# Soft MoE after chunked attention on one core: the scores in two buffers instead of one, and another order of the first loads

## The chip, the core and the metric

The kernel runs on one core of a Trainium2 chip. The core has five engines, each with its own queue of instructions: TensorE (PE, matrix products; PEld is its loading of weights, which overlaps PE), VectorE (DVE), ScalarE (ACT), GpSimd (POOL) and SyncE (SP), which here issues every DMA. [...] The metric is the device time of one execution in microseconds, as the median of several runs.

## The reference

Three stages are computed one after the other, in float32.

```
# 1. attention in chunks of 64: q, k, v are (8, 8, 576, 64)
scores = q_c @ k_c.T / 8 ; attn = softmax(scores) ; x = attn @ v_c      # x: 4608 x 512
# 2. soft MoE: phi 512 x 32, 8 experts with 4 slots each, F = 1024
logits = x @ phi
d = softmax over tokens(logits) ; slots = d.T @ x
slot_out[e] = relu(slots[e] @ w1[e]) @ w2[e]
x = softmax over slots(logits) @ slot_out
# 3. solu block: w_in 512 x 1024, w_out 1024 x 512
h = x @ w_in ; solu = h * softmax(h) ; ln = (solu - mean) / sqrt(var + 1e-6) * g_ln
out = ln @ w_out
```

## The kernel before

The 4608 tokens are 36 tiles of 128 (NT). The first part goes through 36 steps; step i does the attention of tile i and, in the same turn, parts of older tiles. In each step stand, among others:

- `S` (pe_S, L256): eight products of q and k give the scores of tile i, 128 x 512, one PSUM bank. Even steps use one half of the tile `sx`, odd steps the other.
- `mx` (L265) and `sub` (L271) on VectorE: the row maxima, and the scores less the maxima, into SBUF. After `sub` the bank is free again.
- `exp` (L277) on ScalarE; `PT` and `PTe` (L407, L398) transpose the result of the step before on TensorE and copy it out.
- `x` (L282): the product with the values, two steps behind; `rz`, `rc`, `xm` (L304, L483, L487): its sums, their reciprocals, and the scaled x, which frees the two banks of the x tile.
- `xT`, `xTe`, `LT`, `L`, `sl` and others: the transposed x, the logits of a block of four tiles, and the running sums of stage 2.
- `t`, `sq`, `u`, `a`, `m`, `add`, `mul`: from step 2 on, one of 32 conversions a step. The words of w_in and w_out are read as 64-bit pieces (`raw`) and rounded. `t` and `sq` (L210, L206) run on ScalarE, `u` and `a` (L213, L223) on VectorE, `m`, `add`, `mul` (L219, L229, L233) on GpSimd. There is one buffer for what `sq` writes, so `sq` of the next conversion waits for `mul` of this one.

The order of all this is written out by hand in `STEP`, one line for each step modulo 4; each engine executes its share in that order and doesn't overtake. Loads are asked for in the same order on SyncE: `qk` asks for q and k four steps ahead, in two DMAs of 256 KB, `v` for a pair of value tiles (520 KB), `raw` for a pair of words tiles (512 KB), `W` for tiles of the experts' weights (512 KB) as `PACE` says. A DMA waits until the one eight before it has landed. What is asked for before the first step is listed in `FIRST`. Later the hand-written list `ORDER` leads from the last tiles through stage 2 (`x34` uses both halves of `sx` for the values' product of tile 34) into stage 3, which runs tile after tile to the end.

## Time and profile before

| | us |
|---|---|
| median of 3 runs (lowest to highest) | 403.69 (403.28 to 404.21) |
| the profiled execution, its own time | 402.77 |
| span of that execution, first to last instruction | 401.0 |
| PE busy in the span | 382.4 (95%) |
| DVE busy | 311.0 (78%) |
| ACT busy | 224.3 (56%) |
| POOL busy | 200.2 (50%) |

The profile comes from one execution. Its span is 1.77 us shorter than its time, and that time is 0.92 us below the median. Busy shares are means over parts of quite different kinds: attention and conversions until about 124 us, the experts until about 184, the last block until the end. Matrix products are pipelined and their ends are modelled, so two products may overlap in a listing. In every listing, what stands in brackets behind a row is the idle time of that engine just before, and what ended it.

### The profile page before, as it was taken

The page shows a single profiled execution, that of the slowest core. Times are in us where ns is not written, and L with a number is a line of the kernel's source. Part 1 is how long each engine was busy: PE and PEld are TensorE (multiplying, and loading weights), DVE is VectorE, ACT ScalarE, POOL GpSimd, SP SyncE. Part 2 cuts the span into 40 slices and gives each one's busy share as a digit, 9 for nine tenths or more (in the row PEclk, how much of TensorE's full clock was granted, in tenths as well). Part 3 has the DMA queues.
Part 4 walks back from the last instruction along what each step waited for, and adds up shares of the span by engine and source line. Part 5 has one row for each costly group of instructions (what it writes and reads, how often), then busy time and mean ns, then how long its engine had stood idle before and what let it go on. Part 6 is the DMA issues. An engine that isn't in the chain of part 4 may idle for free. (4 is left out here: it accounts for less than half of the span.)

```text
span 401.0 us, 10317 instructions
## 1 busy us (share of the span) xinstructions
PE 382.4 (95%) x3947; PEld 220.4 (55%) x3947; DVE 311.0 (78%) x777; ACT 224.3 (56%) x470; POOL 200.2 (50%) x201
## 2 busy tenths in 40 slices
PE   3799899999999999999999999999999999999997
PEld 2577777777787642354544444444444444444445
DVE  3788788989886449574989799999888888888840
ACT  1577877877785512332577765556554555455521
POOL 2577767777778246330123255555455544454430
PEclk9999999999999999999999999999999999999999
DMA  7999999999999999991156757777665666557671
GB/s 231 403 409 408 389 397 397 409 407 407 410 397 408 401 396 406 409 391 26 30 103 146 140 134 159 159 158 148 144 140 135 144 151 133 132 137 158 132 159 52
DMA packets 101153, 99.20 MB, mean 247 GB/s; under 512 B 78064, under 2 KB 78704, under 8 KB 101104
## 3 DMA queue, kind: packets, MB, share of 16 engines
q1 hardware_dynamic: 101104, 98.54, 77.1%
q8 instruction: 31, 0.51, 0.5%
q14 instruction: 18, 0.15, 0.1%
HBM read 70.60 MB, written 9.44 MB: 200 GB/s over the span
## 5 line engine op out<-in xcount | busy, mean ns | idle before, releaser
L1194 POOL TENSOR_SCALAR uh<-u,sc 128x1024 f16<-128x1024 f32 (+1 forms) x35 | 65.1, 1860 | 51.1 <-issue 38.3
L1393 PEld LDWEIGHTS <-uhT 128*128 128x128 f16 x560 | 52.1, 98 | 68.3 <-issue 8.8
L1393 PE MATMUL o_ps<-xb,uhT 128*128 128x512 f16 x280 | 66.7, 380 | 0.7 <-DMA uhT<-uh 0.7
L1393 PE MATMUL o_ps<-xb,ulT 128*128 128x512 f16 x280 | 66.3, 379 | 0.0
L1393 PE MATMUL o_ps<-wo,uhT 128*128 128x512 f16 x280 | 66.1, 379 | 0.0
L1322 ACT ACTIVATE e<-h_ps,nm 128x1024 f32<-128x1024 f32 x34 | 37.8, 1113 | 43.7 <-DVE nm L1316 43.7
L1210 ACT ACTIVATE e<-u,nmean 128x1024 f32<-128x1024 f32 x35 | 40.1, 1147 | 28.7 <-DVE nmean L1209 28.7
L256 PE MATMUL s_ps<-qk 128*64 128x128 f32 x576 | 41.1, 287 | 9.3 <-DMA qk<-in_qkT 6.5
L1360 POOL TENSOR_TENSOR a<-a,mhalf 128x1 f32<-128x1 f32 x36 | 21.8, 606 | 56.2 <-DVE a L1377 42.5
L1316 DVE TENSOR_REDUCE nm<-h_ps 128x1 f32<-128x1024 f32 x34 | 41.5, 1220 | 9.3 <-PE h_ps L1311 9.3
L1185 DVE SCALAR_TENSOR_TENSOR u<-h_ps,e 128x1024 f32<-128x1024 f32 x35 | 42.8, 1223 | 6.1 <-ACT e L1322 6.1
L1393 PEld LDWEIGHTS <-ulT 128*128 128x128 f16 x280 | 27.3, 98 | 33.1 <-issue 0.3
L1370 DVE SCALAR_TENSOR_TENSOR ul<-u,sc,uh 128x1024 f16<-128x1024 f32 x35 | 45.3, 1295 | 0.0
L256 PEld LDWEIGHTS s_ps<-qk 128*64 128x64 f32 x576 | 32.5, 141 | 16.2 <-issue 10.3
L398 ACT ACTIVATE xt_b<-xt_ps 128x512 f32<-128x512 f32 (+1 forms) x37 | 21.6, 586 | 17.8 <-PE xt_ps L416 16.9
L265 DVE TENSOR_REDUCE mx<-s_ps 128x8 f32<-128x512 f32 x36 | 24.6, 684 | 8.5 <-PE s_ps L256 8.0
L1411 ACT ACTIVATE ob<-o_ps,a 128x512 f32<-128x512 f32 x35 | 23.8, 679 | 9.3 <-PE o_ps L1393 8.0
L219 POOL TENSOR_SCALAR conv<-conv 128x256 f32<-128x256 f32 x16 | 17.6, 1099 | 21.8 <-ACT conv L206 21.8
L1311 PE MATMUL h_ps<-s,c4T 128*128 128x512 f32 x68 | 27.4, 485 | 0.0
L277 ACT ACTIVATE p<-p 128x512 f32<-128x512 f32 x35 | 21.7, 621 | 6.6 <-DVE p L271 6.6
L271 DVE TENSOR_TENSOR p<-s_ps,mx 128x512 f32<-128x512 f32 x35 | 24.1, 690 | 0.9
L229 POOL TENSOR_TENSOR conv<-conv 128x256 int32<-128x256 int32 x32 | 23.3, 729 | 2.6
(232 smaller groups left out, 633.5 us busy)
## 6 DMA issues: line engine op xcount, KB each, us to landing
w<-in_w SPq DMA_DIRECT2D x45, 512.0 KB, 8.0
qk<-in_qkT SPq DMA_DIRECT2D x72, 256.0 KB, 6.8
vall<-in_v SPq DMA_DIRECT2D x18, 520.0 KB, 6.7
out<-ob SPq DMA_DIRECT2D x35, 256.0 KB, 2.1
raw<-in_w SPq DMA_DIRECT2D x16, 512.0 KB, 6.4
qk<-in_w SPq DMA_DIRECT2D x4, 512.0 KB, 9.0
w_raw<-in_w SPq DMA_DIRECT2D x3, 512.0 KB, 9.0
vall<-in_w SPq DMA_DIRECT2D x3, 512.0 KB, 8.9
```

Of the source, the lines that this page charges most:

```text
L256: nc.tensor.matmul(s[ts(c, 64), ts(g, 128)], b[:, 1, ts(2 * g + c, 64)], b[:, 0:3:2, ts(2 * g + c, 64)], start=True, stop=True, tile_posit ...
L265: mark("mx", nc.vector.tensor_reduce(out=mx, in_=s, axis=AX.X, op=ALU.max))
L271: mark("sub", nc.vector.tensor_tensor(out=p, in0=s, in1=mx.unsqueeze(2).to_broadcast([128, 8, 64]), op=ALU.subtract,))
L1185: nc.vector.scalar_tensor_tensor(out=u, in0=d["h"], scalar=1.0, in1=e, op0=ALU.mult, op1=ALU.mult, accum_out=zz[:, 1:2])
L1194: nc.gpsimd.tensor_scalar(out=uh[:, 0:n], in0=u[:, 0:n], scalar1=d["sc"][:, 1:2], scalar2=1.0, op0=ALU.mult, op1=ALU.mult)
L1210: nc.scalar.activation(out=d["e"], in_=d["u"], func=AF.Square, bias=nmean, scale=1.0, accum_out=d["zz"][:, 2:3])
L1311: nc.tensor.matmul(h[:, ts(n, 512)], c4T[:, i, :], s4[n], start=True, stop=True)
L1316: nc.vector.tensor_reduce(out=nm, in_=st[i]["h"], axis=AX.X, op=ALU.max, negate=True)
L1322: nc.scalar.activation(out=d["e"], in_=d["h"], func=AF.Exp, bias=d["nm"], scale=1.0, accum_out=d["zz"][:, 0:1])
L1370: nc.vector.scalar_tensor_tensor(out=ul, in0=d["u"], scalar=d["sc"][:, 1:2], in1=d["uh"], op0=ALU.mult, op1=ALU.subtract)
L1393: nc.tensor.matmul(d["o"], lt(n % 8), w(n % 8), start=(n == 0), stop=(n == 23))
L1411: nc.scalar.activation(out=ob, in_=d["o"], func=AF.Copy, scale=d["a"][:, 7:8])
```

## The change

The score tile with two halves becomes two tiles in a pool of their own. The pool is closed before `x34`, which opens a new one with one tile over two banks; that one is closed before the experts' stage opens its own PSUM pool. In FIRST, q and k of step 3 stand behind g and phi, and the second pair of values and the second and third words are taken out. They are asked for in the `qk` operation of steps 0 and 1 instead, behind q and k of steps 4 and 5. In two lines of STEP `v` moves behind `qk`.

```
-S a x u raw v m qk rz sl mx t W rc z xT sub xTe PT PTe add xm acc mul sq exp
+S a x u raw m qk v rz sl mx t W rc z xT sub xTe PT PTe add xm acc mul sq exp
...
-FIRST = "cs qk0 qk1 qk2 v0 raw0 qk3 g phi v2 raw2 raw4"
+FIRST = "cs qk0 qk1 qk2 v0 raw0 g phi qk3"
+THEN = {0: 'v2 raw2', 1: 'raw4'}
...
-    sx = ps1.tile([128, 2, 512], F32, name="s_ps")
+    pss = ctx.enter_context(ExitStack())
+    ps_s = pool("ps_s", 1, pss, space=PSUM)
+    s_banks = [ps_s.tile([128, 512], F32, name="s_ps", tag=f"s{a}") for a in range(2)]
+    sx = None
 
     def pe_S(i):
-        s = sx[:, i % 2, :]
+        s = s_banks[i % 2]
...
+        def q():
+            load_qk(i + 4)
+            for o in THEN.get(i, "").split():
+                first_loads[o]()
+
...
-            S=(True, lambda: pe_S(i)), qk=(True, lambda: load_qk(i + 4)),
+            S=(True, lambda: pe_S(i)), qk=(True, q),
...
     def x34():
+        nonlocal sx
+        pss.close()
+        sx = pool("ps_sx", 1, pss, space=PSUM).tile([128, 2, 512], F32, name="s_ps")
         xps_t[n - 1] = x = sx
...
     def open_2():
         nonlocal e1, ps2, soT, cz, mx
+        pss.close()
         p1.close()
```

SyncE, from the first load to those of step 2, before. The names ending in 111 to 114 are the four buffers of q and k; 111 is that of steps 0 and 4.

```order
L241 DMA cs_60<-in_cst 128x257
L176 DMA qk0_111<-in_qkT 64x1024 x2
L176 DMA qk1_112<-in_qkT 64x1024 x2
L176 DMA qk2_113<-in_qkT 64x1024 x2
L181 DMA vall_123<-in_v1 128x1040
L189 DMA raw_137<-in_w64 128x1024
L176 DMA qk3_114<-in_qkT 64x1024 x2
L242 DMA g_sb_62<-in_g_ln 128x8
L241 DMA phi_sb_61<-in_phi 128x128
L181 DMA vall_123<-in_v1 128x1040
L189 DMA raw_144<-in_w64 128x1024
L189 DMA raw_146<-in_w64 128x1024
...
```

The same place of the changed kernel, from the first words on:

```order
L190 DMA raw_137<-in_w64 128x1024
L243 DMA g_sb_62<-in_g_ln 128x8
L242 DMA phi_sb_61<-in_phi 128x128
L177 DMA qk3_114<-in_qkT 64x1024 x2
L177 DMA qk0_111<-in_qkT 64x1024 x2
L182 DMA vall_123<-in_v1 128x1040
L190 DMA raw_165<-in_w64 128x1024
L177 DMA qk1_112<-in_qkT 64x1024 x2
L190 DMA raw_182<-in_w64 128x1024
L182 DMA vall_123<-in_v1 128x1040
```

Up to the first words nothing moved. Behind them q and k of step 4 (the second use of 111) now stand ahead of the second values and words, and those of step 5 ahead of the third words.

TensorE around step 7, before, with the semaphores that an instruction waits for (DVE is that of VectorE, the DMAHW ones those of loads):

```order
L256 MATMUL s_ps<-qk_114 64x128 [waits DMAHW2_49,DMAHW1_49,DVE_49]
L256 MATMUL s_ps<-qk_114 64x128 x7
L282 MATMUL x_ps<-vall,pt 64x65 [waits DVE_49,Activation_49]
L282 MATMUL x_ps<-vall,pt 64x65 x15
L356 MATMUL L_ps<-cs,ltb 128x128 [waits Activation_49]
```

And the same instructions of the changed kernel:

```order
L260 MATMUL s_ps<-qk_114 64x128 [waits DMAHW1_49,DMAHW0_49]
L260 MATMUL s_ps<-qk_114 64x128 x7
L286 MATMUL x_ps<-vall,pt 64x65 [waits DVE_49,Activation_49]
L286 MATMUL x_ps<-vall,pt 64x65 x15
L360 MATMUL L_ps<-cs,ltb 128x128 [waits Activation_49]
```

The order on TensorE is the same; the score products have lost their wait for VectorE, and the product with the values behind them has kept its own.

## Rows read from the trace of the kernel before

**Rows 1.** The page's 40 slices of the span: GB/s moved by the DMA engines.

```profile
GB/s 231 403 409 408 389 397 397 409 407 407 410 397 408 401 396 406 409 391 26 30 103 146 140 134 159 159 158 148 144 140 135 144 151 133 132 137 158 132 159 52
```

**Rows 2.** Busy time in stretches: PE, PEld, DVE, ACT, POOL, PEclk, DMA share, GB/s.

```profile
24.00:48.00 24.00, 22.75 (x451) 17.80 (x442) 19.83 (x47) 18.74 (x49) 18.18 (x22) 1.00 1.02 401
48.00:120.00 72.00, 70.27 (x1399) 55.60 (x1397) 62.99 (x162) 54.63 (x146) 54.58 (x63) 1.00 1.02 403
...
160.00:180.00 20.00, 19.29 (x229) 9.02 (x223) 13.90 (x33) 6.66 (x13) 6.99 (x8) 1.00 1.06 404
```

**Rows 3.** The chain that ended last, its first piece: start, us, what.

```profile
202.85 0.80 DVE nm L1316
```

**Rows 4.** Timeline of SyncE, the last weights: start, us, engine, line, operation, tiles.

```profile
147.82 24.39 SPq L128 DMA_DIRECT2D w<-in_w  x22
```

**Rows 5.** The tile w from 171.8 to 172.0 us: its last load, issue to landing.

```profile
L128 SPq DMA_DIRECT2D w<-in_w x1: 328/328/328, 171.9 to 171.9; - x1
...
DMA to landing us min/median/max: 10.4/10.4/10.4
```

**Rows 6.** Timeline of TensorE where the experts' last products stand.

```profile
182.37 0.33 PE L1047 MATMUL soc_ps<-cs,xb 128*128 128x128 f32 x1 [0.44 <-DVE xb L399]
182.63 1.08 PE L987 MATMUL h_ps<-w,hTb 128*4 128x128 f32 x32
183.50 1.06 PE L1112 MATMUL sw_ps<-wi,soT 128*32 128x512 f32 x8
```

**Rows 7.** Waits, 24 to 120 us (PE, then PEld): us in total, times, longest.

```profile
PE s_ps L256 <- DVE p L271: 0.6, 2, 0.3
...
PEld s_ps L256 <- DVE p L271: 3.1, 11, 0.6
...
PEld s_ps L256 <- issue: 2.2, 12, 0.2
```

**Rows 8.** Timeline of all engines around the score products at 32.7 us.

```profile
32.00 0.69 DVE L271 TENSOR_TENSOR p<-s_ps,mx 128x512 f32<-128x512 f32 x1
...
32.74 0.85 PEld L256 LDWEIGHTS s_ps<-qk 128*64 128x64 f32 x16 [0.59 <-DVE p L271]
...
32.90 0.69 DVE L487 TENSOR_TENSOR xb<-x_ps,rz 128x512 f32<-128x512 f32 x1
...
33.77 0.70 PE L282 MATMUL x_ps<-vall,pt 64*64 64x65 f32 x32
```

**Rows 9.** Timeline of all engines, the first three steps.

```profile
5.16 1.97 PE L256 MATMUL s_ps<-qk 128*64 128x128 f32 x16 [5.16 <-DMA qk<-in_qkT]
...
7.90 0.69 DVE L271 TENSOR_TENSOR p<-s_ps,mx 128x512 f32<-128x512 f32 x1
...
8.69 1.98 PE L256 MATMUL s_ps<-qk 128*64 128x128 f32 x16 [1.56 <-DVE p L271]
...
12.55 0.45 ACT L210 ACTIVATE conv<-raw 128x256 int32<-128x256 uint32 x1 [3.30 <-DMA raw<-in_w]
...
12.90 0.58 ACT L398 ACTIVATE pt<-pt_ps 128x512 f32<-128x512 f32 x1
...
13.89 1.09 POOL L219 TENSOR_SCALAR conv<-conv 128x256 f32<-128x256 f32 x1 [11.20 <-ACT conv L206]
```

**Rows 10.** Timeline of all engines, steps 3 to 5.

```profile
17.57 0.42 ACT L210 ACTIVATE conv<-raw 128x256 int32<-128x256 uint32 x1
...
19.39 1.09 PE L256 MATMUL s_ps<-qk 128*64 128x128 f32 x16 [1.01 <-DMA qk<-in_qkT]
...
20.17 0.44 ACT L206 ACTIVATE conv<-raw 128x256 f32<-128x256 f32 x1 [1.10 <-POOL wi L233]
20.17 0.29 DVE L213 TENSOR_SCALAR conv<-raw 128x256 int32<-128x256 int32 x1 [0.62 <-POOL wi L233]
...
23.94 1.07 POOL L219 TENSOR_SCALAR conv<-conv 128x256 f32<-128x256 f32 x1 [0.57 <-ACT conv L206]
```

**Rows 11.** Line 189 from 9.7 to 10.2 us: the second words, issue to landing.

```profile
L189 SPq DMA_DIRECT2D raw<-in_w x1: 457/457/457, 9.8 to 9.8; - x1
...
DMA to landing us min/median/max: 6.9/6.9/6.9
```

## The prediction

> **What bounds the kernel now.** I read the page's slices first, then the busy time by stage, the chain that ended last, and only then the stretches that the change touches. The slices show the loads at 389 to 410 GB/s from the second slice to the eighteenth and 26 in the nineteenth [rows 1]: the weights stream in without a pause until about 182 us. In the same time TensorE is busy for 22.75 of 24 us, then 70.27 of 72, then 19.29 of 20, with the DMA share above 1.00 throughout [rows 2]. So two resources are full at once up to 182 us. The chain that ended last begins only at 202.85 us [rows 3] and is back-to-back TensorE work from there: nothing in it is touched, and it starts earlier only if the stage before ends earlier.

> That stage ends on weights. SyncE asks for the last 22 tiles without rest from 147.82 us [rows 4]; the last one is asked for at 171.9 and lands 10.4 us later, at 182.3 [rows 5]. TensorE uses the last two tiles in the run that starts at 182.63, just after a wait of 0.44 us for VectorE, and goes on at 183.50 [rows 6]. The run takes 183.50 - 182.63 = 0.87 us, half of it for each tile, so the last tile is used from 183.07. If everything on the engines were early, it could be used from about 182.4: **the whole change can win at most about 0.7 us** as long as the last load lands where it does.

> **The change, part by part.** *Two buffers for the scores.* Before, a score product S of a step waits for the subtraction (L271) of the step just before, because both halves are one tile. Afterwards it needs only the subtraction two steps back, which TensorE's earlier wait for the exponential of that step already covers; so S carries no wait for VectorE in the steps. What that frees is read from the waits between 24 and 120 us: weight loads of S that began after L271 sat idle 11 times for 3.1 us in all, against 12 for 2.2 us where nothing held them, 0.18 us each, which is the ordinary gap. The excess is 3.1 - 11 x 0.18 = 1.1 us. By the matmul records the same wait is 2 times, 0.6 us [rows 7]. [...]

> Not all of it reaches the next instruction. The value product x that follows S waits for L487 of an earlier step, which stands on VectorE behind the same subtraction. At the largest stall the subtraction ends at 32.00 + 0.69 = 32.69, S starts at 32.74 after an idle time of 0.59, where 0.17 is the ordinary gap, so it could have started at 32.32; L487 ends at 32.90 + 0.69 = 33.59 and x starts at 33.77 [rows 8]. With S 0.42 us earlier, x could start at best right after 33.59: of 0.42 us some 0.1 to 0.2 remains. So the gain lies between nothing (all of it turned into a wait for L487) and 1.1 us; I take 0.4, about a third, from this row. A loss is excluded for the buffer itself: the two tiles lie in two banks as the halves did, and L487 reading other banks already takes 0.69 us beside S [rows 8]. The same order of release holds where step 34 takes both banks over: it waited for the subtractions of steps 34 and 35 before, too.

> *S of step 1.* It waits 1.56 us for the first subtraction, which ends at 7.90 + 0.69 = 8.59, and starts at 8.69 [rows 9]. That goes; it can start once S of step 0 is through (5.16 + 1.97 = 7.13) and its q and k are there. I cost it at nothing. The cover is the first words: ScalarE stands 3.30 us until they land, converts at 12.55, and only behind that copies the transposed probabilities at 12.90; GpSimd's first conversion follows at 13.89 [rows 9]. The words keep their place in the queue (only smaller or later requests are moved behind them), so 12.55 stays. If that cover were gone the price would be at most the 1.56 us.

> *Order of the first loads.* The second pair of values and the second and third pair of words (0.53 + 0.52 + 0.52 MB) go behind q and k of step 4, the third words behind q and k of step 5. At about 0.4 MB per us [rows 1] that brings q and k of step 4 forward by 1.57 / 0.41 = 3.9 us, and the 1.01 us that S of step 4 waits for them [rows 10] goes. Late instead are the second words: behind 0.52 MB more, 1.3 us. They were asked for at 9.8 and landed 6.9 us later, at 16.7 [rows 11]; now at 18.0. ScalarE wanted them at 17.57 [rows 10], so it waits about 0.4 us, with the sums of x and two copies queued behind it. It then stood idle for 1.10 us until GpSimd released it at 20.17 [rows 10], which swallows the 0.4. And the 1.01 us won on TensorE is swallowed by the same thing: at 20.17 ScalarE and VectorE both wait for GpSimd's multiply, and GpSimd idles only for the 0.57 us of the square that follows [rows 10]. From 13.89 on GpSimd's chain of conversions, one each step, sets the pace of the first steps, and nothing in the change makes it start earlier or run faster. I take 0 for this part, bounds -0.4 (some of TensorE's 1.01 us survives until TensorE becomes the slower one: it is 95% busy from 24 to 48 us and 98% from there [rows 2]) and +0.8 (second rival).

> *The steps' order.* In two of four steps q and k are asked for ahead of the values. Behind 24 us no S waits for q and k any more (the row of waits for them has no entry in that stretch), so this is worth 0; the values come 1.3 us later but are asked for steps ahead.

> **Sum.** -0.4 (score buffers) + 0 + 0 + 0 = -0.4 us, under the cap of 0.7. The profiled execution took 402.77 us with a span of 401.0; it would become 402.4. The median of the three runs, 403.69, lies 0.9 above that execution, and the forecast is for such a median: 403.69 - 0.4 = 403.3 us.

> **Rivals.**
> 1. *The last load lands earlier as well, and all stalls turn into gain.* Then the 1.1 us and the surviving 0.4 pass through. For it: TensorE is nearly full from 48 us on, so what it saves it keeps. Against: the order of requests within a full stream doesn't change when the stream ends, and the bytes are the same. Time: 403.69 - 1.5 = 402.2; with the cap in force it stops at 403.0.
> 2. *The second words come too late.* Their place is the conversion of step 3. The delay passes through once it exceeds the slack of ScalarE there, 1.10 us, against the 0.4 that I work out; from that point each us of delay is a us for GpSimd's chain, which sets the pace. Landing at 19.5 instead of 18.0, they would hold ScalarE for 19.5 - 17.57 = 1.9 us, of which 1.9 - 1.1 = 0.8 come through: 404.5. For it: the first loads take longer than their bytes (the first slice has 231 GB/s [rows 1]). Against: by then the stream is at its full rate.
> 3. *Nothing arrives.* x simply waits for L487 instead of S waiting for L271, GpSimd covers the start: 403.7. For it: rows 8 show S and L487 starting 0.16 us apart; against: the 0.1 to 0.2 us left there.

> **How the numbers follow.** Two measurements of this kernel within 0.2%, 0.8 us, can't be told apart. The forecast (-0.2 to -0.7) has 0.42, the third rival 0.18, the first 0.22 and the second 0.18. The forecast and the third rival lie within the 0.8 us; of the first rival I give 0.03 to the case in which the cap stops it, which lies within too, and 0.19 to the rest; of the second 0.02 to a delay too short to tell, 0.16 to more. So faster 0.19, the same 0.42 + 0.18 + 0.03 + 0.02 = 0.65, slower 0.16. The range: below, the first rival at 402.2 with a little left out, 402.4; above, the second at 404.5 with a little left out, 404.4. The likeliest case alone, with the spread of the three runs about their median (0.4 to 0.5 us each way), is 402.9 to 403.9.

> **What would show it.** Right: S of step 1 starts near 7.9 us instead of 8.69; the first conversions keep 12.55 and 13.89; S of step 4 starts before 18.5 with no wait for q and k; ScalarE waits a few tenths for the second words near 18; weight loads of S no longer wait for L271, and x waits for L487 more often; the last weights land at 182.3 within 0.3 us, and TensorE reaches them a few tenths earlier. Wrong: GpSimd's chain shifted by more than 0.3 us at 24 us, the last load landing earlier than 182.0, or the product of the final stage starting more than 0.8 us before or 0.5 us after its time.

## The result, and the profile after

The changed kernel takes 405.95 us (median of 7 runs, 404.94 to 407.07) against 403.52 us for the kernel before in the same series (7 runs, 402.87 to 405.43): ratio 1.006, 95% interval 1.0035 to 1.0086. It is slower by 2.4 us. 403.3 us was forecast, in a range of 402.4 to 404.4, and "slower" had a chance of 0.16.

The profiled execution took 407.03 us with a span of 405.3. In its page's slices of 10 us the load stream ends later and runs thinner than before, 361 to 409 GB/s between the second slice and the eighteenth [rows 1].

```profile
GB/s 231 406 409 398 381 374 386 397 389 384 399 384 361 406 397 402 408 409 108 3 103 153 134 124 157 158 153 155 155 133 138 155 129 139 133 145 156 131 157 52
```

The busy time of the engines by stretch (columns as in [rows 2]) says where: in the attention steps. From 48 to 120 us TensorE is busy for 66.65 us of 72, 3.6 us less than before, and the loads move 390 GB/s in place of 403. From 160 to 180 us TensorE is as busy as before, 19.29 us.

```profile
24.00:48.00 24.00, 22.12 (x435) 17.36 (x433) 19.66 (x47) 18.38 (x49) 18.26 (x21) 1.00 1.02 393
48.00:120.00 72.00, 66.65 (x1320) 52.06 (x1319) 59.89 (x153) 50.87 (x136) 50.47 (x59) 1.00 1.01 390
160.00:180.00 20.00, 19.29 (x205) 7.41 (x196) 15.38 (x31) 5.46 (x11) 7.99 (x9) 1.00 1.03 409
```

The first 25 us went nearly as written. The timeline (start, us, engine, line, tiles, idle time before and its releaser; compare [rows 9, 10]) has S of steps 0 and 1 in one piece, with no wait for VectorE; the first words at 12.41, GpSimd at 13.75, S of step 4 at 18.36 in place of 19.39, and the conversions that pace the start at 20.24 as before. S of step 6 starts at 24.55, 0.7 us earlier than the 25.27 of before.

```profile
6.05 3.68 PE L260 MATMUL s_ps<-qk 128*64 128x128 f32 x32 [6.05 <-DMA qk<-in_qkT]
...
12.41 0.44 ACT L211 ACTIVATE conv<-raw 128x256 int32<-128x256 uint32 x1 [2.27 <-DMA raw<-in_w]
...
13.75 1.09 POOL L220 TENSOR_SCALAR conv<-conv 128x256 f32<-128x256 f32 x1 [11.05 <-ACT conv L207]
...
18.36 1.09 PE L260 MATMUL s_ps<-qk 128*64 128x128 f32 x16
...
20.24 0.44 ACT L207 ACTIVATE conv<-raw 128x256 f32<-128x256 f32 x1 [1.03 <-POOL wi L234]
```

Then the kernel falls back. The waits of TensorE from 24 to 120 us (us in total, times, longest) no longer name S in the rows of its products: the wait that was removed is gone [rows 7]. New there are three rows whose releaser is "issue", which means that the profile shows nothing that was waited for.

```profile
PE x_ps L286 <- issue: 1.9, 3, 0.8
PE xt_ps L420 <- issue: 1.7, 1, 1.7
PE pt_ps L411 <- issue: 0.8, 1, 0.8
```

The timeline of weight loads shows what is odd in them: TensorE stops inside a group of like instructions, after the first of four transposes at 48.83, and after 21 of the 32 products at 104.12, though nothing new is needed there.

```profile
48.83 0.14 PEld L420 LDWEIGHTS xt_ps<-cs,xb 128*128 128x128 f32 x1
50.60 0.35 PEld L420 LDWEIGHTS xt_ps<-cs,xb 128*128 128x128 f32 x3 [1.64 <-issue]
...
104.12 0.43 PEld L286 LDWEIGHTS x_ps<-vall,pt 64*64 64x64 f32 x21 [0.17 <-ACT p L281]
105.46 0.31 PEld L286 LDWEIGHTS x_ps<-vall,pt 64*64 64x64 f32 x11 [0.91 <-issue]
```

Four such stalls (1.64, 0.86, 1.00 and 0.91 us, ending at 50.60, 71.98, 91.71 and 105.46) make 4.4 us. S of step 35 starts at 128.7 in place of 124.2; it is the second half of the 32 weight loads of this row, first of the kernel before, then of the changed one.

```profile
123.37 1.73 PEld L256 LDWEIGHTS s_ps<-qk 128*64 128x64 f32 x32 [0.17 <-DVE zacc L382]
```
```profile
127.89 1.73 PEld L260 LDWEIGHTS s_ps<-qk 128*64 128x64 f32 x32 [0.17 <-issue]
```

Everything behind it is about as late: the last weights were asked for at 176.2 and landed 10.2 us later, at 186.4 in place of 182.3, TensorE comes to them at 186.73, and the chain that ended last begins 4.1 us later [rows 3 to 6].

```profile
L129 SPq DMA_DIRECT2D w<-in_w x1: 327/327/327, 176.2 to 176.2; - x1
...
DMA to landing us min/median/max: 10.2/10.2/10.2
```

```profile
186.47 0.33 PE L1060 MATMUL soc_ps<-cs,xb 128*128 128x128 f32 x1 [0.44 <-DVE xb L403]
186.73 1.08 PE L1000 MATMUL h_ps<-w,hTb 128*4 128x128 f32 x32
```
```profile
206.95 0.80 DVE nm L1329
```

```profile
q1 hardware_dynamic: 21, 0.08, 102.3%
q8 instruction: 1, 0.02, 32.2%
```

The count is exact. All 8049 instructions of TensorE that the trace lists (its waits for semaphores among them), in order of time, are numbered from 0, and each packet in turn is given 256 of them: in each of the four stalls TensorE has begun 449 instructions beyond the multiple of 256 to which the late packet belongs, never one more. From the 128th of them to the packet's start it takes 5.2 us on average in the kernel before and 6.0 in the changed one (16 packets each, from 26 to 130 us). From the 128th to the 449th TensorE needs 8.2 us in the kernel before, and 2.4 go by after the start; so a packet may start 8.2 - 2.4 = 5.8 us after the 128th instruction before TensorE stops, an estimate from these means. The kernel before is on average just short of that, with 5.2, the changed one beyond, with 6.0. The 128th is a mark for counting; when a packet is asked for the trace does not show. In no run here does a packet start before 152 instructions of its block have begun.

### The profile page after: what moved, and what is told of

Its sections match the earlier page's. It is cut to its first block, busy times and chain, and to the rows that moved or that the text cites. A ratio compares the mean times of both kernels' runs of the same rounds, so it can differ in the third digit from the quotient of the medians.

```text
span 405.3 us, 10335 instructions
## 1 busy us (share of the span) xinstructions
PE 384.6 (95%) x3947; PEld 222.0 (55%) x3947; DVE 311.6 (77%) x777; ACT 224.0 (55%) x470; POOL 200.1 (49%) x201
## 5 line engine op out<-in xcount | busy, mean ns | idle before, releaser
L286 PE MATMUL x_ps<-vall,pt 64*64 64x65 f32 x1088 | 24.9, 227 | 3.1 <-issue 1.9
L220 POOL TENSOR_SCALAR conv<-conv,g_sb 128x256 f32<-128x256 f32 x16 | 18.5, 1157 | 13.9 <-ACT conv L207 13.9
```

What stands on the lines that cost most here:

```text
L220: nc.gpsimd.tensor_scalar(out=m, in0=m, scalar1=1.265625 * 2.0 ** -30, scalar2=g, op0=ALU.is_ge, op1=ALU.mult)
L286: nc.tensor.matmul(x[ts(c, 64), a, ts(g, 65)], pt[ts(a, 64), ts(c, 64)], vall[ts(a, 64), i % 6, ts(2 * g + c, 65)], start=True, stop=True, ...
```

## The experiments

Each kernel is timed in turn with the kernel before; ratios are to that. Four were made for the question which edit it is.

**e1_banks**: the score buffers alone.

```
-FIRST = "cs qk0 qk1 qk2 v0 raw0 g phi qk3"      # in the changed kernel; both STEP lines too
+FIRST = "cs qk0 qk1 qk2 v0 raw0 qk3 g phi v2 raw2 raw4"
-THEN = {0: 'v2 raw2', 1: 'raw4'}
+THEN = {}
```

> The changed kernel with the loads' old order (first loads and both lines of the step order as before): the two score buffers alone. Theories for the 2.4 us that the whole change lost (405.95 against 403.52 us, medians): in the trace of after TensorE stalls four times inside a group of identical instructions (1.6, 0.9, 1.0 and 0.9 us at 50.6, 72.0, 91.7 and 105.5), each time until about 2.4 us after the start of a 16 KB instruction fetch on the DMA engines. Theory A (step order): q and k ahead of v put more loads ahead of the fetches; then this kernel has no such stall and takes 403.0 to 403.6 us. Theory B (score buffers): TensorE, freed from the wait for the subtraction, comes to the end of its fetched instructions sooner; then this kernel has the stalls and takes 405.4 to 406.5 us. Theory C (first loads): where the load stream stands against the fetches is set at the start; then this kernel takes 403.0 to 403.6 us.

Measured: 406.32 us (12 runs, 403.98 to 409.91), ratio 1.0055 (1.0029 to 1.008). The whole loss, with this wait in the profiled execution:

```profile
PE xt_ps L420 <- issue: 0.9, 1, 0.9
```

**e2_loads**: all edits of the loads on the kernel before, one score tile.

> The kernel before with all edits to the loads (first loads and both lines of the step order), its scores still in one tile. Theory A (step order): the stalls inside groups are there, 405.4 to 406.5 us. Theory B (score buffers): no such stall above 0.4 us between 24 and 120 us, 403.3 to 404.0 us. Theory C (first loads): 405.4 to 406.5 us.

Measured: 403.97 us, ratio 1.0003 (0.9987 to 1.0019).

**e3_step**: the kernel before with the two STEP lines of the change.

> The kernel before with only the two lines of the step order changed, q and k asked for ahead of v. Theory A (step order): the stalls inside groups, 405.0 to 406.5 us. Theories B (score buffers) and C (first loads): 403.2 to 403.9 us, no stall above 0.4 us inside a group between 24 and 120 us.

Measured: 404.00 us, ratio 1.0002 (0.9986 to 1.0018).

**e4_first**: the kernel before with FIRST and THEN of the change.

> The kernel before with only the first loads changed: the fourth q and k behind the tables, v and the second and third words asked for behind the q and k of steps 0 and 1. Theory C (first loads): stalls inside groups, 405.0 to 406.5 us. Theories A (step order) and B (score buffers): 403.2 to 404.2 us, no stall above 0.4 us inside a group between 24 and 120 us.

Measured: 403.77 us, ratio 1.0003 (0.9987 to 1.0019). Theories A and C, on the order of loads, fall; B, on the score buffers, stands (e3 lies 0.1 us above its range). One stall above the expected 0.4 us stands in the profiled executions of e2, e3 and e4 too (1.57, 0.68 and 0.65 us), which was expected of none, and the medians don't show it: the kernel before, with one of 0.42, is close to the edge as well.

Next, is it the fetches behind the loads? Two kernels shorten the loads that are out, two thin the stream.

**m1_split_after**, and **m2_split_before** with the same edit:

```
-gated("w", nc.sync.dma_start(out=t[0], in_=w12[m]))
+for k in range(2):
+    gated("w", nc.sync.dma_start(out=t[0][:, k, :], in_=w12[m, :, k]))     # v and raw in the same way
```

> The changed kernel with each load of weights, values and words (0.52 MB) asked for as two halves. Loads share eight semaphores, so at most eight are out at once; with halves there are fewer bytes out when TensorE's 16 KB instruction fetch is asked for (8 x 0.26 MB in place of a mix of 0.26 and 0.52). Theory B, now with its mechanism (TensorE, freed of the wait for the subtraction, reaches the end of its fetched instructions before the fetch, which stands behind the loads that are out): the fetches start 1 us earlier or more, no stall above 0.4 us inside a group between 24 and 120 us, S of step 35 near 124 us in place of 128.8, and 402.9 to 403.8 us. Rival D (two score buffers cost something else, say a different meeting of engines, and the stalls are only where it shows): the time stays at 405.4 to 406.5 us. Rival E: halves make the loads themselves slower; then both this kernel and its twin on the kernel before lose, 405 to 408 us.

> The kernel before with the same loads asked for as two halves. Theory B: 402.9 to 404.0 us, since its stalls inside groups are few. Rival D: 403.4 to 404.2 us. Rival E (halves are slower loads): 405 us or more, with the share of the loads' rate below 395 GB/s between 48 and 120 us.

Measured: 416.18 us, ratio 1.0325 (1.028 to 1.037), and 416.16 us, ratio 1.0288 (1.0251 to 1.0326). Rival E was right on the time. Halves make packets of 2 KB that take 84 ns in place of 160 for 4 KB (medians of queue 1), and from 48 to 120 us the loads move 361 and 378 GB/s:

```profile
48.00:120.00 72.00, 65.42 (x1248) 51.10 (x1243) 57.78 (x148) 50.18 (x134) 49.88 (x58) 0.98 1.01 361
```
```profile
48.00:120.00 72.00, 66.73 (x1328) 52.46 (x1330) 60.66 (x155) 51.60 (x139) 51.99 (x60) 1.00 1.02 378
```

So as a test of B this was badly chosen; what it tells is in the waits. With one score tile the packets came a microsecond earlier (4.2 us on average) and no wait on "issue" is left; with two they came as late as ever (5.9) and the stalls stayed, 2.0, 1.9 and 1.6 us. In the traces of the kernel before and of the changed one at most eight of the 288 DMAs are out at once; in m1, with each of the larger ones halved, the fetches did not come in time by that alone.

**m3_pace_after** and **m4_pace_before**: the weights leave the attention steps.

```
-PACE = [ 0, 0, 0, 0, 0, 0, 0, 1, 2, 2, 3, 4, ... 17, 18, 19, 22, 25, 25, ]
+PACE = [0] * 33 + [22, 25, 25]
```

> The changed kernel, but the first 22 weight tiles are asked for only at step 33 instead of one by one from step 7 on: the loads no longer fill the DMA engines during attention. The whole kernel must take longer, by up to 22 x 1.3 = 29 us, since these weights come later; what counts is the time at which S of step 35 starts. Theory B: fetches start within 2 us of being asked for, no stall above 0.4 us inside a group between 24 and 120 us, and S of step 35 starts at 123.2 to 124.0 us (128.8 with the weights among the steps, 124.3 in the kernel before). Rival D: stalls stay, S of step 35 at 127 to 129 us.

> The kernel before with the weight tiles held back to step 33 in the same way. Theory B: S of step 35 starts at 123.7 to 124.3 us, 0.3 to 0.9 us later than in the changed kernel with the same hold: what the score buffers and the first loads are worth when the fetches do not wait. Rival D: S of step 35 at 124 us here and 127 us or more there.

Measured (one execution each): 425.08 and 425.42 us. The rate falls to 292 and 299 GB/s, DMA share 0.85 and 0.86:

```profile
48.00:120.00 72.00, 70.33 (x1391) 55.44 (x1393) 63.24 (x161) 54.40 (x145) 54.18 (x62) 1.00 0.85 292
```
```profile
48.00:120.00 72.00, 70.65 (x1405) 55.56 (x1401) 63.66 (x163) 55.17 (x147) 55.10 (x63) 1.00 0.86 299
```

S of steps 34 and 35 stands in one group in the timeline of weight loads, first with two buffers, then with one:

```profile
123.86 1.56 PEld L257 LDWEIGHTS s_ps<-qk 128*64 128x64 f32 x28
```
```profile
123.41 1.56 PEld L253 LDWEIGHTS s_ps<-qk 128*64 128x64 f32 x28
```

Step 35 starts at 124.52 against 124.07: the 4.5 us between the two kernels shrink to 0.45, and that is one stall of 0.54 at 70 us. So with the thinner stream most of the loss is gone, in one execution of each. The expectation for m3 (123.2 to 124.0) was missed, because of that stall and because only 0.2 was left at 40 us of the 1.0 us that the two buffers were ahead at 25 us (24.8 against 25.8): x and the transposes wait there for ScalarE instead. With it the expected lead of 0.3 to 0.9 us over m4 was missed. Missed too were fetches within 2 us of being asked for: from the 128th instruction on it takes 4.9 us on average in m3 and 4.0 in m4. The freed wait itself wins TensorE next to nothing.

Where does the freed wait do harm? Three kernels put it back in some steps.

**n1_late** (steps 6 to 33), **n2_early** (steps 1 to 5), **n3_all** (1 to 33):

```
+if g == c == 0 and 6 <= i < 34:          # first product of S; n2: 1 <= i < 6; n3: 1 <= i < 34
+    tc.add_manual_dep(r.ins, LAST["sub"], info, reason="as one tile")
```

> The changed kernel, but from step 6 to step 33 the score product S waits again for the subtraction of the step before, by an added dependency; in steps 1 to 5 it stays free. Where do the freed waits do harm? Theory P (in the first steps: TensorE is 0.7 us ahead at 25 us and the fetches meet the loads otherwise from there on): 405.4 to 406.5 us, with stalls inside groups as in the changed kernel. Theory Q (in the steady steps: each time S is free TensorE runs on to the end of its fetched instructions): 403.3 to 404.2 us, no stall above 0.7 us inside a group between 40 and 120 us.

> The changed kernel, but in steps 1 to 5 the score product S waits again for the subtraction of the step before; from step 6 on it stays free. Theory P (harm in the first steps): 403.3 to 404.2 us. Theory Q (harm in the steady steps): 405.4 to 406.5 us with stalls inside groups.

> The changed kernel with two buffers, but in steps 1 to 33 S waits again for the subtraction of the step before: two tiles that are used as one. If it is the wait and not the place of the buffers that matters, this is as all the load edits with one tile: 403.5 to 404.4 us. If the place of the tiles or their pool costs something, 405 us or more.

Measured: n1 403.64 us, ratio 1.0006 (0.998 to 1.0031); n2 406.35 us, 1.0064 (1.0042 to 1.0087); n3 403.84 us, 1.0007 (0.9987 to 1.0027). Theory Q is right on where the harm arises, in the steady steps, and it is the wait, not the place of the tiles. In n1 the waits of TensorE from 40 to 120 us have S again and no "issue"; in n2 the reverse:

```profile
PE s_ps L260 <- DVE p L278: 0.2, 1, 0.2
```
```profile
PE x_ps L289 <- issue: 0.5, 1, 0.5
```

The profiled execution of n1, which took 1.0 us less than its median, reaches step 35 0.46 us before the kernel before (123.72 against 124.18), of which 0.16 were there by 25 us; the kernel before's own stall of 0.42 near 50 us covers the rest. The last weights land at 182.3 as in the kernel before, and the time is the same within its interval. No version here beats the kernel before.

What S loses by the wait in the steady steps is tiny: its idle time is 0.77 us in four steps with it and 0.70 without. The last three runs ask how so little keeps the fetches in time.

**p1_x**: S free, the next product held instead. **p2_hold23**: S held in the two of four steps in which the subtraction is through long before.

```
+if a == c == g == 0 and 4 <= i < 32:                            # p1, first product of x
+if g == c == 0 and 6 <= i < 34 and i % 4 > 1:                   # p2, first product of S
+    tc.add_manual_dep(r.ins, LAST["sub"], info, reason="...")
```

> The changed kernel with S free in all steps, but from step 6 to step 33 the value product x, the next work of TensorE behind S, waits for the subtraction of the step before. Theory R (any stop that keeps TensorE from running ahead of VectorE by a few tenths in these steps also keeps it from the end of its fetched instructions): 403.3 to 404.3 us, no stall above 0.7 us inside a group between 40 and 120 us. Theory T (it must be S that waits): 405.4 to 406.5 us with stalls.

> The changed kernel with the added wait of S for the subtraction only in steps 6 to 33 whose number leaves 2 or 3 when divided by 4; there the subtraction ends 0.4 to 1.6 us before S starts in the kernel before, so the wait holds nothing. If the waits work by holding TensorE (in the other two steps, where the subtraction ends 0.05 us before S), this one changes nothing: 405.4 to 406.5 us with stalls inside groups. If the mere presence of a wait on the instruction changes how TensorE is fed, 403.3 to 404.2 us.

Measured: p1 406.89 us, ratio 1.0062 (1.0041 to 1.0084); p2 406.56 us, ratio 1.0073 (1.0045 to 1.0101). Both with stalls, p2 the most of all:

```profile
PE x_ps L289 <- issue: 2.0, 2, 1.5
PE xt_ps L423 <- issue: 1.7, 1, 1.7
PE pt_ps L414 <- issue: 1.0, 1, 1.0
```

So a wait that holds nothing does not help (only in step 6 did S stand for it, 0.77 us). That the hold in the other two of four steps would do alone is left to be shown: no run has it by itself. p1 lies 0.4 us above the range of theory T and far from that of R, but its trace has no wait of x for the subtraction (the stalls keep TensorE behind it), so the hold was hardly in force and R is not refuted cleanly.

**p3_qk**: S free; what its end releases is held.

```
 r = nc.sync.dma_start(out=qk[t % 4][a:128:2, a:a + 2, :], in_=qkT[t, a])
+if t >= 10:
+    tc.add_manual_dep(r.ins, LAST["x"], info, reason="q and k behind x")
```

> The changed kernel with S free, but from step 6 on q and k of four steps ahead are asked for only when the value product x behind S is through, about 0.7 us later than the end of S. If S acts on the fetches through the requests it releases (S earlier, q and k asked for earlier, ahead of the fetch in the queue), later requests help: 403.3 to 404.6 us and fetches 0.5 us or more earlier. If it acts otherwise, 405.4 to 407 us with the same stalls.

Measured: 406.33 us, ratio 1.008 (1.0052 to 1.0108), with stalls as before. From the end of S to the requests it takes 1.0 us on average there (steps 8 to 29), 0.4 in the changed kernel and 0.9 in the kernel before; so the requests came as late as before, and the loss stayed. They are not the link either.

All profiled executions together, sorted by whether S is held in the steady steps. The columns are worked out from the traces: start of S of step 35; sum of the stalls over 0.2 us inside groups between 24 us and that start; mean time from the 128th instruction to the packet. The last column is the median. The other columns come from one execution each: those of p1 and p2 were the slowest of their runs (407.94 and 410.16 us).

```
                           S of 35   stalls  packet  median
held  before                 124.2     0.4     5.2    403.5 to 404.1
      e2_loads               125.6     2.0     5.4    403.97
      e3_step                124.7     0.7     5.1    404.00
      e4_first               124.5     0.7     5.2    403.77
      n1_late                123.7     0       5.1    403.64
      n3_all                 124.9     1.4     5.4    403.84
      m2 (halved loads)      130.2     0       4.2    416.16
      m4 (thin stream)       124.1     0       4.0
free  the whole change       128.7     4.4     6.0    405.95
      e1_banks               127.1     1.9     5.4    406.32
      n2_early               126.3     2.6     5.7    406.35
      p1_x                   128.1     5.2     5.9    406.89
      p2_hold23              130.4     6.5     6.3    406.56
      p3_qk                  126.6     3.9     5.7    406.33
      m1 (halved loads)      133.7     5.5     5.9    416.18
      m3 (thin stream)       124.5     0.5     4.9
```

The medians part cleanly: at the full stream, with the loads whole, the six held kernels take 403.5 to 404.1 us and the six free ones 405.95 to 406.89. The columns from single executions don't: e2_loads, held, has 2.0 us of stalls and a packet at 5.4, e1_banks, free, 1.9 and 5.4. So the medians show that the free wait costs time; the stalls show where it went in the executions that were profiled.

## Why the prediction was wrong

**The step that failed** is the lower end of the score buffers: "A loss is excluded for the buffer itself: the two tiles lie in two banks as the halves did". Of the buffers' place this holds (n3 takes 403.84 us, the kernel before 403.79 in its series). But the term was bounded only by waits between engines and by banks, as if a wait less could at worst be worth nothing. The runs show that the buffers alone cost 0.55% (e1), all of it from step 6 on (n2 against n1): in the profiled executions TensorE stands 1.9 to 6.5 us inside groups, waiting, as I read it, for its own instructions. With it fell the premise of the cap, that the last load lands where it does: it landed at 186.4. The rivals had no case for it; the third came nearest in saying that nothing arrives. The 0.16 for "slower" was all for second words that come too late, which did not happen.

**What came out as written**: S of step 1 follows S of step 0; the first conversions keep 12.55 and 13.89 within 0.15 us; S of step 4 starts before 18.5 without a wait for q and k; the second words are in time (rival 2 is out, and e4 agrees); S no longer waits for L271; the loads' orders are worth 0 (e2, e3, e4). Of the other signs, x waiting for the scaled x (L487) more often and the last weights at 182.3 did not come. A slip without weight: 1.57 / 0.41 is 3.8 us, not 3.9.

**Where the gain went apart from the stalls**: of the -0.4 us of the sum some 0.2 is seen, and only from the first steps (0.16 in n1 at 25 us, 0.2 between m3 and m4 at 40 us). These are single executions with the other order of loads as well, so that the buffers won it is not shown. In n1, where the stalls are gone, the last load lands at 182.3 as the cap says.

**A wrong turn in reading.** That weight loads of S idled 1.1 us too long behind L271 [rows 7] was taken for time to be won. In stretches without stalls four steps take 13.8 us with the wait and 13.7 to 13.9 without it: S is idle for only 0.07 us less in them.

**What stays open.** That the stalls wait for instruction packets rests on three things: in all 43 stalls over 0.2 us that the traces of these kernels have inside groups between 24 us and step 35, TensorE stops at the same count, 193 in the next block of 256 (449 - 256); each ends 2.27 to 2.58 us after a packet starts; and with a thinner stream, 292 GB/s in place of 390, 0.5 us of them is left in place of 4.4 (m3). By what so short a hold of S keeps the packets in time is not settled: not by the wait being there (p2), not by the requests for q and k (p3), and smaller loads did not replace it (m1); a hold elsewhere on TensorE was not really tried (p1). That a packet's start depends on which loads are ahead of it is not shown either: no run here moved the packet itself.

## What to carry to other kernels

Here the DMA share was 1.01 to 1.02 and TensorE was busy for 93 to 98% of the time from 48 to 120 us, and the profile counts the 31 packets that I take for TensorE's instructions on the same 16 DMA engines as the loads. In such a kernel look for waits on "issue" inside groups of like instructions, and for the instruction queue in the DMA view, before counting a removed wait as gain. A wait that cost S 0.07 us in four steps parted 403.5 to 404.1 us from 405.95 to 406.89 here, so a bound of "at worst nothing" needs a reason for each resource that the faster engine uses up sooner. And when a change has several edits, test them one by one: of the three groups of edits here the two to the loads did nothing.

## What was not expected of the hardware

While the kernel runs, packets of 16 KB come on a queue named "instruction", 31 in the execution; by the count above one goes with 256 of TensorE's instructions, and that they bring these instructions is my reading. Between 24 and 121 us 15 of them stand in the kernel before and 15 in the changed one, 6.5 and 6.7 us apart on average, each 0.92 to 1.11 us long.

Where the stream was thinnest a packet started 1.2 to 1.9 us after the 128th instruction (four packets of m4 between 94 and 115 us; 276 GB/s from 92 to 116 us); under the full stream it was 4.1 to 6.1 us in the kernel before and 3.0 to 7.2 in the changed one (16 packets each, from 26 to 130 us). The packets do not simply wait for what was asked for before: in the changed kernel the last of the loads asked for by the 128th instruction lands between 1.4 us before the packet's start and 3.1 us after it (the same 16 packets). The packet at 103.11 us comes 6.9 us after the 128th instruction, and the words that were asked for 0.65 us after that instruction land by 103.13. What sets the start of a packet is not shown.
